# Three-stage attention and gated-MLP kernel: first query tiles issued from ScalarE, another order of the front

## The chip, the core and the metric

The kernel runs on one core of one Trainium2 chip. The metric is device time in microseconds (us) of that core. Inside the core PE (TensorE) does matmuls and transposes, DVE (VectorE), ACT (ScalarE) and POOL (GpSimd) do elementwise work, and SP (SyncE) issues DMAs. Each engine works through a queue of its own in order; a waiting instruction holds up all that stand behind it on its engine.

## What is computed

Attention with a sliding window of 16 and, beside it, one summary key and value for each block of 32; then a gated layer with a spatial matrix; then a second layer with a convolution of three taps.

```python
def _attn_ref(q, k, v):            # B=2, H=8, S=768, D=64
    k_sum = k.reshape(B, H, nb, 32, D).max(axis=3)
    v_sum = v.reshape(B, H, nb, 32, D).mean(axis=3)
    scores_l = scale * q @ k.T;  masked to abs(i - j) < 16
    scores_s = scale * q @ k_sum.T + log(32)
    a = softmax(concat(scores_l, scores_s))
    return a @ concat(v, v_sum)
def _moe_ref(x, ...):              # d_model 512, d_ff 1024
    u, v = halves of relu(x @ w_in)
    return (u * (w_spatial @ layernorm(v) + b_spatial)) @ w_out
def _moe2_ref(x, ...):
    h = relu(x @ w_in);  return (h * sigmoid(conv3(h))) @ w_out
```

## The kernel before

The attention is cut into 8 head pairs n (four for each of two batches) and each pair into two groups of six blocks of 64 queries, so there are 16 groups i. What is here called the front is the first 40 us or so: the groups of the first pairs, the loads of their keys, queries and values, and the conversion of the first weights. From then on matmuls of the gated layer ("dense" work) fill the PE between the groups.

One group (function group, L488 on) is a chain over four engines: scores on PE (L496, L503 and 24 matmuls of L509), the row maximum on DVE (L513), six exponentials with their sums on ACT (L517), the sum and its reciprocal on DVE (L520, L523), the scaling on POOL or DVE (L526), two lots of three transposes on PE (L530), each followed by a copy out of PSUM on ACT or DVE (L552), the product with the values on PE (L536), and the result split into a high part (L557, ACT or DVE) and a low part (L558, DVE). Scores of even and odd groups use two PSUM buffers in turn: scores of group i wait for the exponentials of group i - 2. All transposes share one PSUM bank, so a second lot waits for the copy of the first.

Ahead of a pair's scores stand its keys (function keys): two scaled windows of the keys, one for each group (L422 on ACT, L424 on DVE or POOL), the block maxima ("tops", L432 on DVE; two for each early pair) and their spread into place (L438). The values' block means (function means) are matmuls for pairs 0 and 2 (L452) and a DVE sum with a transpose for the others (L459, L462); ACT or DVE takes them out of PSUM (L464), and L469 (ACT) or L471 (POOL) spreads them. The first weight w_in comes in eight pieces of 64-bit words; each is converted by a scaling (L307 on ACT, L308 on POOL), three bit operations on DVE (L310, L312, L314), a cast (L298) and a subtraction (L292). The scaling takes the piece straight from its DMA.

Sizes of the loads follow from their shapes (128 partitions, 4 bytes an element): a pair's keys come as 416 and 384 columns (208 and 192 KB), its queries as two halves of 384 columns (192 KB each), its values as two pieces of 288 KB, a piece of w_in is 256 KB. All loads of before are issued by SP (L397 keys, L400 queries, L410 and L406 values, L306 weights).

The order of the work is not found by the compiler. Each job is given to a plan with add(); two tables written out in the file then decide: ORDER lists all jobs in the order in which they are emitted, two characters a job, and so sets each engine's queue; PICK says for each job that may run on several engines which one it takes. Where the plan's own estimate sees a gap of 0.5 us or more on PE it puts in filler matmuls (L1085, bf16 ones, result unused). Seven filler matmuls also stand at the very start. The estimate is used for nothing else on the chip.

Before the plan's jobs stand two DVE memsets and one exponential on ACT of a single column (L1080), which makes ACT load its table.

Of the kernel before, what the change touches and what calls it, by code (L numbers as in the profile page):

```python
# [59 lines left out]
    "EtDpEuC7C8C9C+C-BXEiDqDBCLFiEvFjE3E4EjEkDzD0EwFvCMCNDuDvCOCPD6DCDDDED7D8D9D1D+D2EEEFD3FBCQEGE5EmDFDGFkEHEIE6D4F6F7EOEPEQ"  # L60
    "ERGmD5F8F9C4FCD-EAEBECFWEXE7FFFGEYEZEaEbGnFHFIFJFKElFXEDE8GlEcEdE9FYFLGkFZFlFaGQGRGDE+ExEJEKELESHPGSGEGFEyFmE-FAFnEzFbFz"
    "F0EMFwGtG6GdEVJwFQFRFcFdF1ENHHHIGeF2F3GfGGGgF4FeHQFSFTF5FoHJFUHRGhGiGjFpFqFrGuFDG7HSHTHKHLEWFsG8GTGUGHF+GVGIFtHMHNFuFfFg"
    "HiHjFxHkHlGJFyG9G+HOHUHXHYGvGKGwHZHVFhHmHWIhGLGMF-GxGyGAHyGBHnIDHzHaGWGXImGCH0FEGoH1HbHcGYHoHqGNGZGaGbHrHsGOGcGPHdG-JtGz"
    "JuIrItIuHtIcG0H2HeGpG1HuIdIiHfIwH3GqG2IsM-INGrJxIOJzGsHvJ3HAIPHBIIHgH4HCInHDG3NBHwG4HEG5IjIvHFIXJ6IJHhJ0IEIYIKNAJ4HGNCIQ"
    "JvIeH5IZJ1IaIbIRIkIFJ5IfIxJyIyIzJBHxJCISJDHpIgILH8I0H+KbJ2H6KBJ8IlITNNKCJEH9H-IMI5H7NDKFI6IBI1I7KDIUIAIoI8JRKcJFKGI9J7NG"
    "NJJGICKHIVKXJ9JHNII2I+I3JSIWJTJUKAKYI-JJJVJIJZJaI4J-JbNEJAJcIpJKKIJWJhKEJLJdJMNFKJNHIqLDJiJeNKLHJXNUJNKQJfIGJjJ+KKJOIHKd"
    "KhJYKRJPJgLIJQKiJmKLLJJoKjNQKSJkKeNLJnLEJpJlJrLFKfKzKlKsKmKtJsKuK0KnKgKZKaLLKMLMK9KTNPLKNMK5LGKkK7LPNOLNK-K+LTNbNRKNLQNS"
    "K6NTNWLXLRLBKvLUNXLOK8LYLZLbKONVNYLVLSNiLcLdNZLALfLgLWNdLeLaKoNeLhLiNaLlLzNcKPNfLCLoL2NpLjKpNgLmNhLpNkL3NlNjLnLkL0L4MOMB"
    "NmJqKqMPMcNnKUMHL1NrNoMQNsNwKrLrNqMINtK1MEMJMRL5MCNuKVMVMdMFNzNvLqNyPXMWKWN3PLMXMDNxK3L6KwL7N0MYN1MeMmPYMnN5K4MfPMMsN2N6"
    "MGK2N4N7LvN+PZPNPaKxN8MoKyN9OAOBMKL9MzMtLsLwN-OCPbMjMuOFPOODPdOHM0PROILxPPMLMkPSOEM7OGOJMpLtPvMqPTMlMrOMPeL+OKPfPQMvOOOL"  # L70
    "OPONOTM3L-MwMxP1P2PpM4OQOUPjMMPkPUPcOaOROWMyLyOVOSMSPlOhPqM5MgM8PVPgP3PWM1MAPmMhOcM9PrOdObM6P7LuP4MZM2MiP8PnQFOXOeM+MaP5"
# [1161 lines left out]
```

## Time and profile before

| | us |
|---|---|
| median of 3 runs | 320.15 (319.69 to 320.52) |
| the profiled execution | 320.81 |
| span of its trace | 318.9 |
| PE busy in the span | 311.4 (98%) |

The span runs from the first to the last instruction of the trace; 1.9 us of the profiled execution lie around it. Busy PE time includes the filler matmuls. The views used are the busy time by engine, the busy time in stretches of the span (for all of an engine's work and for the filler alone), the instructions in order of time with what ended their waits, and the list of who waited for whom.

### The profile page before, as it was taken

How to read it: one execution, taken by the hardware profiler on the slowest of the kernel's cores; microseconds unless marked ns; L12 is line 12 of the kernel's file. 1: busy time of each engine (PE TensorE's matmuls, PEld its weight loads, DVE VectorE, ACT ScalarE, POOL GpSimd, SP SyncE). 2: the span in 40 equal slices, each digit the busy share in tenths (PEclk: the TensorE clock that was granted, in tenths of full speed). 3: DMA queues.
4: the chain of work that ended last, by engine and by line, in shares of the span. 5: the costliest groups of instructions: out<-in, count | busy, mean ns of one | idle time of the engine just before them, and what ended most of it. 6: DMA issues, size and time to landing. Idle time of an engine off the chain costs nothing.

```text
span 318.9 us, 6374 instructions
## 1 busy us (share of the span) xinstructions
PE 311.4 (98%) x2376; PEld 271.6 (85%) x2376; DVE 268.5 (84%) x493; ACT 237.3 (74%) x565; POOL 117.0 (37%) x130
## 2 busy tenths in 40 slices
PE   7899999999999999999999999999999999999994
PEld 3677889888888888999998888888888899999994
DVE  6789899886677978988987797799999999989971
ACT  3999888978385735677987687998788997684721
POOL 3597853804235337255532332210110222254010
PEclk9999999999999999999999999999999999999999
DMA  7999875935453000114434343400110412154432
GB/s 222 305 266 306 224 218 179 329 93 159 168 189 110 24 2 13 53 29 142 138 114 124 117 134 133 132 2 0 25 21 5 75 25 51 26 99 104 128 140 99
DMA packets 16061, 37.64 MB, mean 118 GB/s; under 512 B 1952, under 2 KB 8480, under 8 KB 16032
## 3 DMA queue, kind: packets, MB, share of 16 engines
q1 hardware_dynamic: 13728, 34.11, 35.0%
q0 software_dynamic: 2304, 3.15, 5.7%
q8 instruction: 18, 0.29, 0.4%
q14 instruction: 11, 0.09, 0.1%
HBM read 30.96 MB, written 3.15 MB: 107 GB/s over the span
## 4 chain that ended last, share of the span: by engine, by line
PE 88%; DVE 5%; DMA 2%; SPq 1%; ACT 1%; POOL 1%; issue 1%; DVEq 0%; POOLq 0%
PE late L345 11%; PE late L346 11%; PE late L344 11%; PE mm L344 10%; PE mm L346 9%; PE mm L345 9%; PE pt L530 3%; PE xp L344 3%; PE xp L346 3%; PE xp L345 3%; PE xp L536 3%; PE pt L344 3%; PE pt L346 3%; PE pt L345 3%; PE s L509 2%; DMA a<-q_in 2%
## 5 line engine op out<-in xcount | busy, mean ns | idle before, releaser
L517 ACT ACTIVATE a<-s,a 128x120 f32<-128x120 f32 x96 | 33.3, 379 | 1.0 <-DVE a L513 0.8
L345 PE MATMUL late<-xl,a 128*128 128x512 f32 (+1 forms) x80 | 29.5, 369 | 0.1
L344 PE MATMUL late<-xh,a 128*128 128x512 f32 (+1 forms) x80 | 29.4, 367 | 0.0
L346 PE MATMUL late<-xh,a 128*128 128x512 f32 (+1 forms) x80 | 29.4, 367 | 0.0
L914 DVE SCALAR_TENSOR_TENSOR w<-v,conv_t,w 128x1534 f32<-128x1534 f32 x12 | 21.8, 1817 | 4.4 <-POOL w L908 2.1
L876 POOL DMA_DIRECT2D tmp<-w x9 | 8.4, 931 | 42.5 <-ACT tmp L875 31.1
L526 POOL TENSOR_TENSOR a<-a,a 128x720 f32<-128x720 f32 x14 | 19.4, 1394 | 6.4 <-DVE a L523 3.5
L517 ACT ACTIVATION_READ_ACCUMULATOR a<-s,a 128x1 f32 x96 | 21.6, 225 | 0.0
L292 POOL TENSOR_TENSOR w<-a,w 128x256 fp32r<-128x256 f32 (+2 forms) x13 | 14.2, 1099 | 15.1 <-PE late L345 7.9
L530 PE MATMUL pt<-ident,a 128*120 128x128 f32 x96 | 16.5, 281 | 0.8 <-DVE a L552 0.6
L345 PEld LDWEIGHTS late<-xl,a 128*128 128x128 f32 x80 | 15.0, 188 | 2.4 <-DVE xl L292 0.4
L346 PEld LDWEIGHTS late<-xh,a 128*128 128x128 f32 x80 | 15.0, 188 | 1.9
L344 PEld LDWEIGHTS late<-xh,a 128*128 128x128 f32 x80 | 15.0, 188 | 1.8
L513 DVE TENSOR_REDUCE a<-s 128x6 f32<-128x720 f32 x16 | 14.2, 899 | 2.2 <-PE s L509 2.1
L298 ACT CAST w<-a 128x512 fp32r<-128x512 f32 (+2 forms) x17 | 10.0, 589 | 7.9 <-DVE a L337 3.4
L327 ACT ACTIVATE a<-a 128x512 uint16<-128x512 uint8 x20 | 15.8, 789 | 0.0
L330 ACT ACTIVATE a<-a 128x512 f16<-128x512 f32 x20 | 15.6, 782 | 0.0
L298 ACT CAST xh<-tmp 128x384 fp32r<-128x384 f32 x24 | 12.1, 512 | 3.9 <-DVE tmp L878 2.0
L530 PEld LDWEIGHTS pt<-ident,a 128*120 128x120 f32 x96 | 10.8, 137 | 5.0 <-DVE a L552 1.0
L344 PE MATMUL mm<-w,xh 128*128 128x512 f32 x36 | 14.9, 414 | 0.0
L344 PE MATMUL mm<-xh,a 128*128 128x512 f32 (+1 forms) x40 | 14.7, 367 | 0.0
L346 PE MATMUL mm<-xh,a 128*128 128x512 f32 (+1 forms) x40 | 14.7, 367 | 0.0
(399 smaller groups left out, 1130.8 us busy)
## 6 DMA issues: line engine op xcount, KB each, us to landing
a<-w_in SPq DMA_DIRECT2D x8, 512.0 KB, 3.5
a<-w_out SPq DMA_DIRECT2D x8, 512.0 KB, 3.5
a<-vhalf SPq DMA_DIRECT2D x8, 288.0 KB, 6.9
a<-v_in SPq DMA_DIRECT2D x6, 384.0 KB, 6.8
a<-vwin SPq DMA_DIRECT2D x4, 576.0 KB, 6.9
a<-w_in SPq DMA_DIRECT2D x8, 256.0 KB, 7.1
a<-w_inv SPq DMA_DIRECT2D x4, 512.0 KB, 4.1
a<-w_outT SPq DMA_DIRECT2D x4, 512.0 KB, 3.6
```

Source lines behind the costliest of these rows:

```text
L292: eng.tensor_tensor(out=lo.r(), in0=src.f(), in1=hi.f(), op=ALU.subtract)
L298: us = {"ACT": (0.2 + n / 1200, lambda: ACT.copy(hi.r(), src.f())), "POOL": (0.12 + n / 1050, lambda: POOL.tensor_copy(hi.r(), src.f()))}
L327: ACT.activation(out=c.ap.bitcast(U16).rearrange("p (n w) -> p n w", w=2)[:, :, 0], in_=byte, func=AF.Copy, scale=1.0 / 32.0, bias=-15.5 / ...
L330: ACT.mul(c.ap.bitcast(F16).rearrange("p (n w) -> p n w", w=2)[:, :, 1], word(), 2.0 ** -60)
L344: PE.matmul(ps, lhsT=lh, rhs=rh, start=first and i == 0, stop=False, **kinds)
L345: PE.matmul(ps, lhsT=lh, rhs=rl, start=False, stop=False, **kinds)
L346: PE.matmul(ps, lhsT=ll, rhs=rh, start=False, stop=last and i == n - 1, **kinds)
L513: DVE.tensor_reduce(out=st[:, 0], in_=sv, op=ALU.max, axis=AX.X, negate=True)
L517: ACT.activation(out=e[:, u, :NK], in_=sv[:, u // GA, u % GA], func=AF.Exp, bias=st[:, 0, u:u + 1], accum_out=sm[:, u, :1])
L526: eng.tensor_tensor(out=e, in0=e, in1=st[:, 1].unsqueeze(2).to_broadcast([128, GB, NK]), op=ALU.mult)
L530: PE.transpose(pt3[:NK, a], e[:, GA * h + a, :NK], ident)
L914: DVE.scalar_tensor_tensor(out=two(ct)[:, bs, to], in0=two(h)[:, bs, of], scalar=scale(k), in1=two(ct)[:, bs, to], op0=ALU.mult, op1=ALU.add)
```

## The change

- The two DMAs of pair 0's queries leave SP's queue and become the first two instructions of ACT's queue.
- The exponential that loads ACT's table becomes a job of the plan behind these two DMAs; the copy of the "one" tile comes after it.
- On SP's queue the second half of w_in's first chunk (issued third before) goes behind the first values; pair 1's keys move ahead of both.
- ORDER and PICK are new: 62 jobs take another engine, and the queues of PE, DVE, ACT and POOL are in another order up to the second layer's start. SP's queue is the same from the second values piece on.

```diff
             q0, q1 = S // qp * i, S // qp * (i + 1)
-            dma((q1 - q0) / 2 * 0.84 + (166 if n + i == 0 else 0), lambda ...: SP.dma_start(qts[j].ap[:, q0:q1], q_in[b, p][:, q0:q1]), r - 9 + 1.5 * i, writes=[...])
+            if n:
+                dma((q1 - q0) / 2 * 0.84, lambda ...: SP.dma_start(qts[j].ap[:, q0:q1], q_in[b, p][:, q0:q1]), r - 9 + 1.5 * i, writes=[...])
+            else:
+                add({"QA": (1.2 - 0.4 * i, lambda ...: ACT.dma_start(qts[j].ap[:, q0:q1], q_in[b, p][:, q0:q1]))}, r - 100 + i, writes=[...])
...
-    ACT.activation(out=stat[0][:, 11:12], in_=mhalf, func=AF.Exp)
...
+    def table():
+        ACT.activation(out=stat[0][:, 11:12], in_=mhalf, func=AF.Exp)
...
-    add({"ACT": (2.65, one_tile)}, -99, [tok("ident")], [mask_b.tok(sub="o")])
+    add({"ACT": (2.2, table)}, -99.5, writes=[tok("table")])
+    add({"ACT": (0.6, one_tile)}, -99, [tok("ident"), tok("table")], [mask_b.tok(sub="o")])
```

ORDER and PICK, read back into jobs, give these queues. A job is named with its pair (n) or group (i); k, q, v are loads, a and b their first and second piece; w(c, part) is a piece of w_in.

```
SP before:   k0a k0b w(0,1) q0a k1a k1b q0b v0a w(0,0) q1a v0b k2a k2b q1b ...
SP after:    k0a k0b k1a k1b v0a w(0,1) w(0,0) q1a v0b k2a k2b q1b ...      ACT: q0a q0b

ACT before:  table, one, win0/1, cast w(0,1), exp0, scale w(0,0), exp1, win2/0, exp2, mean-out0,
             copy0/1, cast w(0,0), exp3, exp4, copy2/0, hi1, copy2/1, exp5, copy3/1, scale w(2,0),
             exp6, scale w(1,0), exp7, mean-out2, spread2/0, hi3, copy4/1, win4/1, copy5/0,
             spread2/1, copy5/1, exp8, copy6/0, mean-out3, spread3/0, cast w(1,1), copy7/0,
             scale w(3,0), hi6, exp9
ACT after:   q0a, q0b, table, one, win0/0, win0/1, win1/0, exp0, scale w(0,0), exp1, cast w(0,1),
             win2/0, exp2, cast w(0,0), copy0/1, exp3, hi0, exp4, win3/0, hi1, copy2/1, exp5,
             spread1/0, copy3/1, win4/0, exp6, copy4/0, scale w(2,0), mean-out2, hi3, copy4/1,
             exp7, hi4, exp8, hi5, copy6/0, win5/0, copy6/1, spread3/0, copy7/0, spread3/1, hi6,
             copy7/1, exp9

PE before:   filler, s0, s1, mean0a, s2, mean0b, t0, s3, t0', s4, t1, pv0, t1', t2, s5, pv1, t2',
             s6, t3, mean1, t3', dense(256), s7, pv2, t4, mean2a, mean2b, t4', pv3, s8, dense(512),
             t5, pv4, t5', s9
PE after:    filler, s0, s1, mean0a, s2, mean0b, t0, s3, t0', s4, t1, pv0, t1', s5, t2, pv1, t2',
             s6, t3, mean1, mean2a, t3', s7, pv2, t4, mean2b, pv3, t4', s8, t5, pv4, t5',
             dense(512), s9

DVE before:  constants, win0/0, masks, top0a, top0b, put0, w(0,1) x3, max0, top1b, top1a, max1, ...
DVE after:   constants, masks, top0a, top0b, put0, top1a, max0, top1b, max1, w(0,1) x2, sum0, ...
```

## Rows read from the trace of the kernel before

**Rows 1.** Page, part 1: busy us, share of the span, instructions of each engine.

```profile
PE 311.4 (98%) x2376; PEld 271.6 (85%) x2376; DVE 268.5 (84%) x493; ACT 237.3 (74%) x565; POOL 117.0 (37%) x130
```

**Rows 2.** Stretches A:B: length, each engine's busy us (instructions), granted clock, DMA share, GB/s.

```profile
0.00:5.00 5.00, 3.96 (x11) 1.48 (x12) 2.70 (x23) 2.54 (x5) 1.85 (x11) 1.00 0.61 185
5.00:10.00 5.00, 4.01 (x73) 2.11 (x71) 3.31 (x8) 2.12 (x12) 2.82 (x5) 1.00 1.00 277
```

**Rows 3.** Who waited for whom on PE from 12 us on: total, times, longest.

```profile
PE pt L530 <- DVE a L552: 0.6, 1, 0.6
PE s L509 <- DMA a<-q_in: 0.3, 1, 0.3
```

**Rows 4.** In order of time, ACT's start and first issues: start, us, engine, line.

```profile
0.72 1.28 ACT L1080 ACT_TABLE_LOAD   x1 [0.72 <-PEq L1226]
0.73 0.86 SPq L397 DMA_DIRECT2D a<-k_in  x2
...
1.63 0.42 SPq L306 DMA_DIRECT2D a<-w_in  x1
...
2.10 0.43 SPq L400 DMA_DIRECT2D a<-q_in  x1
```

**Rows 5.** In order of time, the first users of loads: the bracket is the wait ended.

```profile
3.80 0.68 ACT L422 ACTIVATE a<-a 128x576 f32<-128x576 f32 x1 [1.18 <-DMA a<-k_in]
...
5.77 0.29 DVE L310 TENSOR_SCALAR a<-a 128x256 uint32<-128x256 uint32 x1 [0.40 <-DMA a<-w_in]
...
6.44 0.84 PE L509 MATMUL s<-a,a 64*64 64x120 f32 x24 [0.57 <-DMA a<-q_in]
...
10.89 0.45 ACT L307 ACTIVATE a<-a 128x256 f32<-128x256 f32 x1 [0.44 <-DMA a<-w_in]
...
12.09 0.85 PE L509 MATMUL s<-a,a 64*64 64x120 f32 x24 [0.34 <-DMA a<-q_in]
```

**Rows 6.** In order of time, from the second block maxima to the first exponentials.

```profile
4.48 0.54 DVE L432 TENSOR_REDUCE a<-a 128x12 f32<-128x384 f32 x1
...
5.06 0.31 DVE L438 TENSOR_SCALAR a<-a 128x288 f32<-128x288 f32 x1
...
8.29 0.36 ACT L517 ACTIVATE a<-s,a 128x120 f32<-128x120 f32 x1 [0.59 <-DVE a L513]
...
10.22 0.23 ACT L517 ACTIVATION_READ_ACCUMULATOR a<-s,a 128x1 f32 x1
```

**Rows 7.** Stretches between instructions of the front, columns as in rows 2.

```profile
10.89:41.94 31.05, 29.70 (x536) 23.23 (x534) 27.00 (x64) 28.86 (x123) 24.36 (x30) 1.00 0.91 259
12.09:35.52 23.43, 22.53 (x420) 17.53 (x421) 20.55 (x49) 21.83 (x97) 18.86 (x23) 1.00 1.01 296
```

**Rows 8.** The second stretch of rows 7, filler matmuls alone: PE, PEld busy.

```profile
12.09:35.52 23.43, 1.03 (x4) 0.39 (x4) 1.00 1.01 296
```

**Rows 9.** ACT's groups by shape, 10.89 to 41.94: busy us, mean ns, idle before.

```profile
L552 ACT COPY a<-pt 120x384 f32<-120x384 f32 x9 | 4.4, 485 | 0.7 <-PE pt L530 0.5
L469 ACT COPY a<-a 24x768 f32<-24x768 f32 x3 | 2.5, 829 | 0.1
L307 ACT ACTIVATE a<-a 128x256 f32<-128x256 f32 x4 | 1.9, 466 | 0.4 <-DMA a<-w_in 0.4
L557 ACT CAST xh<-xp 128x384 fp32r<-128x384 f32 x3 | 1.4, 480 | 0.8 <-PE xp L536 0.7
L422 ACT ACTIVATE a<-a 128x576 f32<-128x576 f32 x2 | 1.4, 684 | 0.0
L298 ACT CAST w<-a 128x256 fp32r<-128x256 f32 x2 | 0.8, 408 | 0.0
L464 ACT ACTIVATE a<-mm 24x128 f32<-24x128 f32 x2 | 0.5, 265 | 0.0
```

**Rows 10.** In order of time on PE, one dense step of 256 columns and what follows.

```profile
25.27 0.36 PE L344 MATMUL mm<-xh,w 128*128 128x256 f32 x1
...
25.81 0.23 PE L496 MATMUL s<-a,ones 64*64 64x72 bf16 x4
```

More of the change, by code (lines that the diff above doesn't have):

```diff
@@ L60 @@
[L60 to L71, printed above, removed]
@@ new lines @@
+    "EgBfCrBJBgBhChEiBLB3BNBKBMBiCsDTCtCXB4DfBOBtAZB5BPEfBuBvDUCiCjASCFCYC3CuDgCGB6CZBUCkCHB7DVB8DWBQClCaCICbEoCvCBCmDhCwEpCx"
+    "DsEUDiCnEqCLE1DXBRCyCoCzDYDtC0CJDjDNFPC1C4DZDaFNDbDOErDkDxCCEsDyDPDlDQDBDmC6CKDzEjFQDcEtE2AgDnFODRDuC8DdCDC7DoDeEVEuE3BV"
+    "C9DpC+BWFWDqFwBXEvE4FCDrFjEwCMC-C5EkFDE5DAD0ElD1CNE6CODvD7BYExCPFkDDDwDCF7D8D9D+DEDFCQD-E7CRF9FlE8D2EFEYDGD3D4EZD5GmD6DH"
+    "FXEGEaFGFYE9F+EbEHEcEAFmE+FHEBF8F0EIEJFIECFJFZEDGEGRFxGlFnFKEnFaE-EmFbEEEyEPGFGnEdEQFAERFBFcGSGGESEzGeEKEWEeGoF2ELFoFdET"
@@ new lines @@
+    "FRFeFLF1E0EMHQFSJxENFEGTFMFfF3FpGUHRF4GgFqGfG7GhF5GuGHEOEXGiFrHIGVFTHJF6HKFUFsGjGIFVGvHSGkG8HLHTGwFyF-GJFgHUFtFhHMFzFiG9"
+    "FuHjGAFFGxHkFvHYIdGKGBJuGLIeHlGMGyGDInGNHmIsGpGWGCGXHnIuGYIvGzHZHNHaG+G-GZIoGaHVHzGbGOHbHAGcGPGdIxG0IpHWGQG1GqH0G2HcHXIf"
+    "HOItG3H1NAGrHdHBIiIwHrHeHPGsHCHDHfJ0HEHsH2HgHoGtHFG4H3IJJ1JyIKHGHHIgITIUILJ2IMIVJ4IqHtJzJ6HhNCHuNBH4G5IWIhKCG6IjIkH5HvIl"
+    "ImHwKDKEH6NDHxKGHiKHKIIOHpNOHyIEHqIYIPIXH-INI6H9IFJ5IrNEJ3J7JKH+IZIaNHKYKcH7IQIGJ9IRJ8KZISI7KdIbJCIAIcKFJDIyNFI8I9IzICI+"
@@ new lines @@
+    "H8J+I-I0I1IDIBI2JEJFJAI3JaJGNGJSNIJTNJI4JBJUJVI5JbJLJHNKJIJWJcJdJJJiJeJXJMJNKKJjJONLKJJfJYJkKLJgKRJPKeNRJQJZJhJRJlJnKfKS"
+    "JpLIKMKgJmJoKTNQIHLEKhKaKmJqKtIINMKbLFK0JsNNJtKiKjNPKnKkNSK6KoKlKuK1NTKvK+K8LJNUK-LQLGK9LMLNLHLKLLLRK7LOLSLPLTNVLUNYNXLA"
+    "KANWNcLVLcNjLYLdKBNZLWJ-LeKNJvNaLBKULgKOLhLZLXLaKPNeLCLfLbKpNfLiLjNbLmL0KwNdKQNgLDLpL3NqLkKqNhLnNiLqNlL4NmNkLoLlL1L5MPMC"
+    "NnJrKrMQMdNoKVMIL2NsNpMRNtNxKsLsNrMJNuK2MFMKMSL6MDNvKWMWMeMGN0NwLrNzPYMXKXN4PMMYMENyK4L7KxL8N1MZN2MfMnPZMoN6K5MgPNMtN3N7"
@@ new lines @@
+    "MHK3N5N8LwN-PaPOPbKyN9MpKzN+OBOCMLL+M0MuLtLxOAODPcMkMvOGPPOEPeOIM1PSOJLyPQMMMlPTOFM8OHOKMqLuPwMrPUMmMsONPfL-OLPgPRMwOPOM"
+    "OQOOOUM4MAMxMyP2P3PqM5OROVPkMNPlPVPdObOSOXMzLzOWOTMTPmOiPrM6MhM9PWPhP4PXM2MBPnMiOdM+PsOeOcM7P8LvP5MaM3MjP9PoQGOYOfM-MbP6"
+    "PiPtOlMcQBQHQCPxMOOkL9QDOgOjPjMUMVOpQIQETYQJP+OZJwOrOsOqTZOmPuOtQKP-OhPyTeQFQAOnOwPpOuO3PzTfOvPvQYOzP7QZOyQLQdQMQeQNOxO0"
+    "QaO5QbO+O6QfO4P0QcQTQUOoQVQgO7QOQPPAOaQhQWRGO1RBPFQXQQQiPBO8PHO-QvPGP1QRQ0O9O2RLQjQkQ1Q2QqTaQwPCQrQSPIQsQtQ3PJQlQxTbQyTk"
@@ new lines @@
+    "TgRCRMQmQuRHRdQ4ThQzRDQnQ5TqTsRERNRIRYRJRORZQ6TmRaVARiRjQ7TtQoPDReTiRFR3QpTcRKRtRyTjTrRPRuRQTdUxRbTlTnT3UyRRQ8RkRzRfQ9Tu"
+    "RSRgTvR0RlR4T4UsPKRUQ+RvPLR5RTR1ToRcQ-RhRmRwR6U2RnSHSMSNT7TpRASCRVSgSDR2RxR7PETwTxR8SEU3SFRoSIRWRpRrRqSGU7R9SJR+R-SAUzSO"
+    "SKSbSLScShRXSPRsU8SdVBSBTDSiSRTQTSSeSQTRU9SSSUSlSTTIU0SVSjSWUtS0SmS+SXVCU4U1SnSfS5TTUuSoTKSYVLSZSkSqVMTLSaTyS6TJVESrSpSs"
+    "VDTES1UvStS-U+VFS2S3TMVNSuSvSwVWSyS7S8TUUYVPVHTNTVSxU5USUMUeTOS4UmUNVQSzVIU6UZTFUfUTVOUgTAUwT5S9TPUOVXUaVGVhVSUUVYWBVZVs"
@@ new lines @@
+    "UkU-TWVdTGViUVVTV8UWUPVeTBWCT8VJUQV9V4V0V5VRUqVKTHVuVjVaVUTXVkVoV1VcWxV2UoWyV6VVTzT0VfVwV7VpV3VnV+VgWDVlT+WEWzXAWFXBV-UA"
+    "UbT6WAUFW2VbWsWNWOW3WGXCUHVmUBWHUnWIUIW0W1WPUlWQWtT1WJVqUhXLVrVtUrWRUiXMWaUpWKT2XETCWbW7W4WLWUWuXNUcW5XDWvWcXFW8WwXHXIXW"
+    "XPWVWdW9W6WWXOXQXhWXXwXXXYX0XSX4YBWSX5WgT-XGVvX8XTX1T9X6WmUCXZW+YCXiWTXdUdXaUDW-VyXRXjXsWnXeXkX2VxX9WhXoUEX3XJYDX7XpVzUG"
+    "X+WiYEXlYFXuXKX-WoYAXmYNXbYOWYYGUJWMYHURWeUKXcULYPXvYIXyXtYJXUWpYQYKXfYUYLXVYRXxYSWjXzWqXnXqWkYaYgYmXgYnUjYhUXWZYMYoYTYp"
@@ L399, in load_kq @@
             q0, q1 = S // qp * i, S // qp * (i + 1)
-            dma((q1 - q0) / 2 * 0.84 + (166 if n + i == 0 else 0), lambda q0=q0, q1=q1: SP.dma_start(qts[j].ap[:, q0:q1], q_in[b, p][:, q0:q1]), r - 9 + 1.5 * i, writes=[qts[j].tok(q0, q1)])
+            if n:
+                dma((q1 - q0) / 2 * 0.84, lambda q0=q0, q1=q1: SP.dma_start(qts[j].ap[:, q0:q1], q_in[b, p][:, q0:q1]), r - 9 + 1.5 * i, writes=[qts[j].tok(q0, q1)])
+            else:
+                add({"QA": (1.2 - 0.4 * i, lambda q0=q0, q1=q1: ACT.dma_start(qts[j].ap[:, q0:q1], q_in[b, p][:, q0:q1]))}, r - 100 + i, writes=[qts[j].tok(q0, q1)])
     def load_values(n):
```

22 lines of the change are left out of this document (5 added, 17 removed).

## The prediction

> **What bounds the kernel now.** I read the busy time by engine first: PE is busy for 98% of the span [rows 1], so what a change of the front can win is time in which PE does nothing useful. Next I read the list of PE's waits after 12 us: apart from 0.3 us for queries and 0.6 us for a copy on DVE it holds nothing worth a tenth per cent [rows 3]. The matmuls after the front are dense, so each microsecond by which the front's useful PE work is done sooner should reach the end of the run, and each new hole in it too. The loss is thus in the front, and in two parts. Up to 12.09 us PE does scores of two groups and half a block mean; the second pair's queries end that part [rows 5]. From 12.09 us to the tenth group's scores (s9) at 35.52 us, PE is busy for 22.53 of 23.43 us, of which 1.03 us is filler [rows 7, 8]: 21.50 us of work, 1.93 us lost.
>
> Then I asked what else is full there. The DMA engines are: their share is 1.00 from 5 to 10 us, at 277 GB/s, after a first stretch of 0.61 that includes the time before the first issue at 0.73 us [rows 2, 4]. ACT is nearly full: from 10.89 us, when a piece of w_in lets its scaling start [rows 5], to the start of exp9 at 41.94 us it works for 28.86 of 31.05 us and is idle for 2.19 us [rows 7]. So two limits stand beside PE: the bytes that must land, and ACT's one queue.
>
> **The change, part by part: the queries on ACT's queue.** Before, the first query piece was issued at 2.10 us behind keys and a weight piece, and s0's big matmuls started with it at 6.44 us after a wait of 0.57 us [rows 4, 5]. Now it is issued at about 0.7 us beside the first keys. No trace shows a DMA issued from ACT; the nearest rows are SP's 0.43 us each [rows 4]. Twice that is 0.86 us ahead of the table load, which moves from 0.72 to about 1.6 us. ACT's first need of data came at 3.80 us after a wait of 1.18 us [rows 5], so this is hidden; with that cover gone it would cost 0.86 us.
>
> What the queries gain, the keys lose. Both key pieces, 400 KB, had landed by 3.80 us, three pieces (656 KB) by 5.77 us, four (848 KB) by 6.44 us [rows 5]. Now 784 KB compete (two of keys, two of queries). Let L be the landing of the second key piece. Read off between 656 KB and 848 KB, L is 6.27 us; counted from 400 KB at 3.80 us with 277 GB/s [rows 2, 5], 0.393 MB take 1.42 us and L is 5.2 us. I take the middle, 5.75 us. From it the chain is: block maxima and spread, 4.48 to 5.37 us before [rows 6], 0.89 us; s0 and the row maximum, from 6.44 to 8.29 us [rows 5, 6], 1.85 us; exp0, 8.29 to 10.45 us [rows 6], 2.16 us; together 4.90 us. So s0's matmuls start at 6.1 to 7.2 us (before 6.44), and exp0 ends at L + 4.9, that is 10.1 to 11.2 us. s1 no longer waits, and follows.
>
> **What does not move.** Behind exp0 on ACT stands, before and after, the scaling of w(0,0), and behind that exp1. The scaling started at 10.89 us, when its piece landed [rows 5]. In the old order the pieces up to and with it are k0a, k0b, w(0,1), q0a, k1a, k1b, q0b, v0a, w(0,0), 1984 KB. In the new order they are the same nine pieces, on two queues. With the same DMA engines full, the piece lands at the same time and exp1 starts at about 11.24 us again, provided that exp0 is done, which holds for L below 5.99 us; at L = 6.27 us it is 0.28 us late. The second pair's queries, 192 KB behind, also have the same bytes ahead of them, so s2 stays at about 12.09 us. What is won ahead of 12 us by earlier s0 and s1 is then lost again in these two waits: I count it at nothing, with 0.28 us of loss as the other bound, and a gain as in the first rival.
>
> **The new order after that.** The most it can win by s9 is the 1.93 us lost there now. ACT's queue decides how much comes, since s9 needs the buffer that exp7 reads. In the new order there stand from exp1 to exp7 seven groups of exponentials at 2.16 us (15.1), two casts at 0.41 (0.8), three key windows at 0.68 (2.1), five copies at 0.485 (2.4), three high parts at 0.48 (1.4), one spread at 0.83, one scaling at 0.47 and one mean at 0.27 [rows 6, 9]: 23.4 us. Without any hole exp7 ends at 11.24 + 23.4 = 34.7 us, and s9 starts then. Before, s9 started at 35.52 us, but PE had done one dense step of 256 columns more, 0.54 us from 25.27 to 25.81 us [rows 10]. So the gain is 35.52 - 34.7 - 0.54 = 0.3 us. If ACT's neighbours overlap by about 0.1 us each it is more; a hole on ACT makes it less. It lies between 0.9 and -0.5 us, which I take from half a microsecond of such overlap or of holes on either side.
>
> The other moved jobs are costed at nothing: the three bit operations of w(0,1) on DVE wait for a piece that lands four us later, but only the cast on ACT behind exp1 and dense steps after 30 us need them. POOL has ten jobs fewer; DVE gets them, with 268.5 us busy of 318.9 us [rows 1]. If DVE lost that cover, each moved job would cost some 0.4 us (its bit operation takes 0.29 us [rows 5]).
>
> **Sum.** The profiled execution took 320.81 us, 318.9 us of it span; the 1.9 us around it stay. 318.9 - 0.3 = 318.6 us of span, 320.5 us in all. That execution is 0.66 us above the median of the runs, 320.15 us, so the forecast median is 320.15 - 0.3 = 319.85, say 319.9 us.
>
> **Rivals.** First, the queries on a queue of their own cost the others nothing, and all that SP issues lands sooner. The nine pieces then count 1600 KB; 384 KB at 277 GB/s [rows 2] are 1.4 us, ACT's chain starts at about 9.8 us, and the gain is 1.7 us: 318.4 us. For it speaks the share of 0.61 in the first five us, part of which may be room that a second queue fills; against it the full 1.00 right behind [rows 2]. The Trainium skill ("DMA: Bandwidth & Descriptors", section "Issuing engines are not separate DMA queues") says that DMAs of ACT and SP run on the same 16 engines and interleave, and that a second issuer saves issue time only. It speaks against this rival, as the full share does; by it the sum stays at the forecast.
>
> Second, the slower side: ACT becomes the bound. Between exp1 and exp9 the new queue holds, against the old, three high parts (1.44), three windows (2.05), two spreads (1.66), three copies (1.46) and a cast (0.41) more, 7.0 us, and two means (0.53), three copies (1.46), two scalings (0.93), two spreads (1.66), a window (0.68) and a cast (0.41) less, 5.7 us, by the same durations [rows 9]. That is 1.35 us more. ACT was idle for 2.19 us there [rows 7]; if the new order leaves it idle for more than 0.84 us, exp9 comes later than at 41.94 us, and if it is idle for as long as before, by 1.35 us, with PE's transposes behind it: 320.15 + 1.35 = 321.5 us. For it speaks that most of ACT's idle time was waiting for PE's transposes and products [rows 9], which a new order need not remove; against it that PE has dense steps between its groups from 33 us on.
>
> Third, the change does not do what it says: the table load goes first and the queries are issued at about 2 us, as before [rows 4]. The keys then land as before, and the bound by w(0,0) is the same: 320.1 us, with the order's part alone.
>
> **Chances.** Forecast 0.45, first rival 0.25, second 0.22, third 0.08. About 0.3%, 0.96 us, can be told from no change, so the borders are 319.2 and 321.1 us. Faster: 0.05 of the forecast and 0.22 of the first rival, 0.27. Slower: 0.04 of the forecast and 0.16 of the second, 0.20. Within: 0.53. The range from 318.4 to 321.5 us takes in the sum's ends (319.2 to 320.7) and reaches to the centres of both rivals.
>
> **What would show it.** Right, if the scaling of w(0,0) starts within 0.4 us of 10.89 us and s2 within 0.4 us of 12.09 us, with the keys' second piece at 5.2 to 6.3 us and s9 at 34 to 35.5 us. The first rival shows in a scaling at about 9.5 us; the second in ACT idle for over 0.84 us between them and exp9 past 42 us; the third in a table load ahead of the DMAs. I am wrong if PE's waits or filler after 36 us exceed half a microsecond, or if s0's 24 matmuls take much over 0.84 us at a granted clock of 1.00 [rows 2, 5], since less filler stands before them.

## The result: slower

| | before | after |
|---|---|---|
| median of 6 runs, us | 320.53 (319.69 to 322.13) | 323.98 (322.49 to 327.81) |
| the profiled execution | 320.81 | 324.33 |
| span of its trace | 318.9 | 322.4 |

The ratio after to before is 1.0102 [1.0056, 1.0148]; it leaves out the run of 327.81 us, which fell in a slower state. The brackets are intervals of 95%. A second measurement of the unaltered changed kernel, in the last experiment, gave 322.38 us and 1.0054 [1.0029, 1.0079]. The two overlap between 1.0056 and 1.0079; I take it that the change costs somewhat over half a per cent. The forecast was 319.9 us with a range up to 321.5 us, and it put the likeliest outcome at no change that can be told.

First the page of the changed kernel, part 1 (busy us, share, instructions), which answers [rows 1]:

```profile
PE 313.8 (97%) x2382; PEld 271.9 (84%) x2382; DVE 279.5 (87%) x503; ACT 236.8 (73%) x565; POOL 110.2 (34%) x120
```

PE is busy 2.4 us longer with 6 instructions more: fillers, 28 instead of 22. DVE has ten instructions more and is busy 11.0 us longer; POOL has ten less and is busy 6.8 us less. These are net numbers. The two PICK tables differ for 66 jobs (not 62, as the section on the change has it): 17 go from POOL to DVE and 9 back, 14 from ACT to DVE and 12 back, 8 from POOL to ACT and 6 back. So 11.0 against 6.8 us is not the price of ten jobs.

Then the loads, in order of time, against [rows 4, 5]; the bracket is the wait that the instruction ended with:

```profile
0.72 0.89 ACTq L403 DMA_DIRECT2D a<-q_in  x2
0.72 1.80 SPq L397 DMA_DIRECT2D a<-k_in  x4
1.64 1.28 ACT L1116 ACT_TABLE_LOAD   x1 [1.64 <-PEq L1232]
...
4.81 0.56 DVE L435 TENSOR_REDUCE a<-a 128x12 f32<-128x384 f32 x1 [0.70 <-DMA a<-k_in]
...
5.40 0.31 DVE L441 TENSOR_SCALAR a<-a 128x288 f32<-128x288 f32 x1
...
11.64 0.46 ACT L307 ACTIVATE a<-a 128x256 f32<-128x256 f32 x1
```

The second key piece had landed at 4.81 us, and the keys' maxima were in place at 5.71 us. The scaling of w(0,0) at 11.64 us no longer waits for its DMA: it follows the six exponentials of exp0 without a break. The stretches of [rows 2], for the changed kernel (length, busy us by engine, granted clock, DMA share, GB/s):

```profile
0.00:5.00 5.00, 3.96 (x10) 1.48 (x11) 2.19 (x22) 2.74 (x6) 1.85 (x11) 1.00 0.64 212
5.00:10.00 5.00, 5.00 (x80) 2.98 (x79) 2.49 (x6) 1.56 (x5) 0.67 (x1) 1.00 1.04 321
```

In ten microseconds 2.67 MB are moved (5 x 212 and 5 x 321), against 2.31 MB before. The front is better fed; how much of this is the change and how much the execution, the queries alone show below. What PE does with it stands in its own timeline:

```profile
1.04 6.66 PE L1087 MATMUL mm<-ones 128*128 128x512 bf16 x17 [1.04 <-DVE mhalf L1082]
...
7.81 0.79 PE L512 MATMUL s<-a,a 64*64 64x120 f32 x24
...
11.83 0.23 PE L499 MATMUL s<-a,ones 64*64 64x72 bf16 x4 [0.29 <-ACT a L520]
...
11.99 0.81 PE L512 MATMUL s<-a,a 64*64 64x120 f32 x24
```

Seventeen fillers stand ahead of s0, where before had thirteen, and they last until 7.70 us. The keys had been ready for two microseconds by then. So s0 starts at 7.81 us (6.44 before [rows 5]), exp0 at 9.62 us (8.29 [rows 6]), and s2 waits for exp0's buffer. Who waited for whom on PE from 12 us on (total, times, longest), against [rows 3]:

```profile
PE mm L455 <- DMA a<-vhalf: 1.0, 1, 1.0
PE xp L465 <- DVE xl L561: 0.9, 1, 0.9
PE xp L539 <- issue: 0.4, 1, 0.4
PE xp L539 <- DVE a L526: 0.4, 1, 0.4
PE late L344 <- DVE a L751: 0.3, 1, 0.3
PE s L499 <- ACT a L520: 0.3, 1, 0.3
PE pt L533 <- ACT a L555: 0.2, 1, 0.2
```

That is 3.5 us. [rows 3] hold 0.9 us, and the same list of before has a third row, 0.2 us for values, so 1.1 us in all. The two largest are a block mean that waits for its values at 25.68 us and a transpose of pair 5's value sums at 67.22 us that waits for DVE. The stretches that answer [rows 7], for ACT from the scaling to exp9 (11.64 to 44.08 us) and for PE from s2 to s9 (11.99 to 37.10 us):

```profile
11.64:44.08 32.44, 30.30 (x536) 23.33 (x535) 29.77 (x68) 29.96 (x126) 23.82 (x28) 1.00 0.77 228
11.99:37.10 25.11, 23.26 (x436) 17.69 (x432) 23.32 (x54) 22.99 (x105) 19.22 (x23) 1.00 0.93 269
```

And the filler alone in the second, as in [rows 8]:

```profile
11.99:37.10 25.11, 2.24 (x8) 0.62 (x8) 1.00 0.93 269
```

From s2 to s9 filler fills 2.24 us instead of 1.03 us. Last, what goes on around the wait at 67.22 us, DVE and POOL in order of time:

```profile
63.49 1.58 POOL L292 TENSOR_TENSOR w<-a,w 128x512 fp32r<-128x512 f32 x1
...
63.83 2.00 DVE L529 TENSOR_TENSOR a<-a,a 128x720 f32<-128x720 f32 x1
65.76 0.94 DVE L462 TENSOR_REDUCE a<-a 128x24 f32<-128x768 f32 x1
66.62 0.54 DVE L561 TENSOR_TENSOR xl<-xp,xh 128x384 fp32r<-128x384 f32 x1
...
67.22 0.28 PE L465 MATMUL xp<-ident,a 128*24 128x128 f32 x1 [0.90 <-DVE xl L561]
```

The scaling of group 11 (L529) was POOL's before; the new PICK gives it to DVE. There it takes 2.00 us beside a subtraction on POOL. Behind it on DVE's queue stand the value sum (L462) and a low part (L561), and PE's transpose waits for these.

### The profile page after: what moved, and what is told of

It reads as the page before. It is cut to its first block, busy times and chain, and to the rows that moved or that the text cites. A ratio compares the mean times of both kernels' runs of the same rounds, so it can differ in the third digit from the quotient of the medians.

```text
span 322.4 us, 6405 instructions
## 1 busy us (share of the span) xinstructions
PE 313.8 (97%) x2382; PEld 271.9 (84%) x2382; DVE 279.5 (87%) x503; ACT 236.8 (73%) x565; POOL 110.2 (34%) x120
## 4 chain that ended last, share of the span: by engine, by line
PE 76%; DVE 12%; ACT 4%; POOL 3%; issue 2%; DMA 2%; DVEq 0%; POOLq 0%; ACTq 0%
PE late L345 9%; PE late L344 9%; PE late L346 9%; PE mm L344 8%; PE mm L346 7%; PE mm L345 7%; PE pt L533 3%; PE mm L1087 2%; PE xp L539 2%; PE xp L345 2%; PE xp L346 2%; PE xp L344 2%; PE pt L346 2%; PE pt L344 2%; PE pt L345 2%
## 5 line engine op out<-in xcount | busy, mean ns | idle before, releaser
L345 PE MATMUL late<-xl,a 128*128 128x512 f32 (+1 forms) x80 | 29.5, 369 | 0.1
L346 PE MATMUL late<-xh,a 128*128 128x512 f32 (+1 forms) x80 | 29.4, 367 | 0.0
L520 ACT ACTIVATION_READ_ACCUMULATOR a<-s,a 128x1 f32 x96 | 22.5, 234 | 0.0
L529 POOL TENSOR_TENSOR a<-a,a 128x720 f32<-128x720 f32 x12 | 16.8, 1400 | 15.1 <-DVE a L526 11.2
L345 PEld LDWEIGHTS late<-xl,a 128*128 128x128 f32 x80 | 15.0, 188 | 2.3 <-DVE xl L292 0.4
L346 PEld LDWEIGHTS late<-xh,a 128*128 128x128 f32 x80 | 15.0, 188 | 1.9
L555 ACT COPY a<-pt 120x384 f32<-120x384 f32 x20 | 9.8, 491 | 8.5 <-PE pt L533 8.2
L346 PE MATMUL mm<-xh,a 128*128 128x512 f32 (+1 forms) x40 | 14.7, 367 | 0.0
L345 PE MATMUL mm<-xl,a 128*128 128x512 f32 (+1 forms) x40 | 14.7, 367 | 0.0
```

The costliest lines, as they stand in the source:

```text
L345: PE.matmul(ps, lhsT=lh, rhs=rl, start=False, stop=False, **kinds)
L346: PE.matmul(ps, lhsT=ll, rhs=rh, start=False, stop=last and i == n - 1, **kinds)
L520: ACT.activation(out=e[:, u, :NK], in_=sv[:, u // GA, u % GA], func=AF.Exp, bias=st[:, 0, u:u + 1], accum_out=sm[:, u, :1])
L529: eng.tensor_tensor(out=e, in0=e, in1=st[:, 1].unsqueeze(2).to_broadcast([128, GB, NK]), op=ALU.mult)
L555: (ACT.copy if eng is ACT else DVE.tensor_copy)(part.ap[:NK], pt[:NK, :128 * GA])
```

## The experiments

The theories were these. **Filler:** the plan's own estimate puts seventeen fillers ahead of s0, four more than before, and the front's gain is spent on them. **Order:** the new ORDER and PICK make holes later, whatever the front does; within it, the wait at 67 us and the values at 25 us were suspects. **Loads:** the queries on ACT's queue delay or speed the other loads, and with them the scaling of w(0,0). **Clock:** with less filler PE's slow start costs as much as the filler did. In the expectations quoted below, Theory A is Filler, B and F are Order, C is Loads, D is filler and order together, and G is Clock. Each ratio below is to the kernel before on the same chip. In the diffs, FILLS replaces the estimate by fixed numbers of fillers, by job; job 43 is s0, and seven more fillers stand at the very start in all kernels.

### Less filler ahead of s0 (e1_filler), and the changed kernel without the new queue (e2_order_alone)

```diff
# e1: the changed kernel
+FILLS = {43: 3, 99: 3, 49: 3, 156: 2, 107: 3}
-                if self.fill and gap >= 0.5:
-                    n = int((gap - 0.1) / 0.22)
+                if self.fill and FILLS.get(k, 0):
+                    n = FILLS.get(k, 0)
# e2: the changed kernel, 17 fillers (43: 10), and
-            if n:
+            if True:   # pair 0's queries by SP too; loads and table load in before's order
```

> The changed kernel with 3 instead of 10 filler matmuls added behind the seven of the start, so 10 instead of 17 stand before the first scores; all else, the later filler too, is as in the changed kernel. Theory A (the filler holds the front): in the changed kernel the keys were spread at 5.71 us, but the first big score matmuls started at 7.81 us behind 17 fillers; here they start at 5.9 to 6.1 us, exp0 at about 7.8 us instead of 9.62 us, exp1 at 11.0 to 11.4 us instead of 11.97 us, and the time falls by 0.6 to 1.5 us, to 322.5 to 323.4 us. Theory B (the new order behind 12 us loses the time): s0 starts sooner, but the time stays within 0.5 us of 323.98 us.

> The changed kernel's order and engine choices with the loads as before: the first queries on SP's queue again, the piece of w_in third; the numbers of filler matmuls are those of the changed kernel (17 before s0). Theory B (the new order loses the time): 323 to 325 us, with the hole on PE ahead of the third pair's block means (0.96 us) and that at 66 us (0.9 us) still there. Rival C (the loads lose it, because keys, values or weights land later): back to 320.0 to 321.0 us.

e1 took 321.49 us, 1.0031 [1.0015, 1.0047], a larger gain than Theory A expected; e2 took 323.24 us, 1.0075 [1.0048, 1.0101], as Theory B expected. In e1 everything in front comes sooner (PE and ACT in order of time):

```profile
1.04 3.68 PE L1088 MATMUL mm<-ones 128*128 128x512 bf16 x10 [1.04 <-DVE mhalf L1083]
...
5.85 0.85 PE L513 MATMUL s<-a,a 64*64 64x120 f32 x24 [0.84 <-ACT a L426]
...
9.73 0.45 ACT L308 ACTIVATE a<-a 128x256 f32<-128x256 f32 x1
...
10.07 0.81 PE L513 MATMUL s<-a,a 64*64 64x120 f32 x24
```

s0 is two microseconds sooner than in the changed kernel, s2 too, and s9 starts at 33.76 us against 35.70 us before. Yet the kernel is slower than before. So filler is a part of the loss and not all of it, and what else costs lies behind s9. e2 says that it does not hang on the queue: with the old loads the new order is slower all the same.

### The queries alone (e3_queries_alone, e7_queries_filler)

```diff
# e3: the kernel before with the change's q0a, q0b and table jobs; old order of all else, 13 fillers
-SP: k0a k0b w(0,1) q0a k1a k1b q0b v0a ...   ACT: table, one, ...
+SP: k0a k0b w(0,1) k1a k1b v0a ...           ACT: q0a, q0b, table, one, ...
# e7: e3 with 10 fillers ahead of s0
```

> The order and engine choices of before with nothing but the first queries moved to ACT's queue ahead of the table load; the piece of w_in stays third on SP's queue, the filler numbers stay those of before (13 in front of s0). Theory B: 319.8 to 320.8 us, no change; s0 starts at 5.6 to 6.4 us instead of 6.44, s2 at 12.1 us as before. Rival C (the queries' loads cost the rest): 321.5 us or more, with s2 later than 12.6 us. A third view (they help by themselves): below 319.6 us.

> e3_queries_alone (the order of before, the first queries on ACT's queue) with 10 instead of 13 filler matmuls in front of s0. Theory A in its general form (filler in front of s0 costs as soon as the scores could start before it ends, and how long it takes depends on when PE's clock rises in that execution): 319.7 to 320.4 us, and the times spread less than the 319.97 to 322.20 us of e3_queries_alone. Rival: the filler is hidden there, 320.5 to 321 us with the same spread.

e3 took 320.70 us, 1.0001 [0.9976, 1.0026], as Theory B expected; e7 took 320.31 us, 1.0007 [0.9978, 1.0037], and its times spread over 319.71 to 323.05 us, where a smaller spread than e3's was expected. These are e3's stretches up to 10 us:

```profile
0.00:5.00 5.00, 3.96 (x12) 1.52 (x13) 2.26 (x23) 1.94 (x5) 1.85 (x11) 1.00 0.64 210
5.00:10.00 5.00, 4.87 (x84) 3.06 (x81) 4.59 (x10) 2.48 (x11) 3.01 (x5) 1.00 1.05 319
```

The trace of before alone is not enough to compare with. In e8, below, all loads are issued by SP in the order of before and only the filler differs; its stretches are:

```profile
0.00:5.00 5.00, 3.96 (x11) 1.49 (x12) 2.72 (x23) 2.54 (x5) 1.85 (x11) 1.00 0.60 164
5.00:10.00 5.00, 5.00 (x81) 2.94 (x80) 3.64 (x9) 1.97 (x10) 3.10 (x5) 1.00 1.02 319
```

All traces together, one for each kernel:

| first queries issued by | traces | 0 to 5 us, GB/s | 5 to 10 us, GB/s | MB in 10 us |
|---|---|---|---|---|
| SP | before, e2, e6, e8 | 141 to 185 | 277 to 331 | 2.31 to 2.42 |
| ACT | the 13 others | 210 to 218 | 295 to 361 | 2.52 to 2.89 |

So the issue from ACT feeds the first five microseconds better in every trace, by 0.26 MB in the mean (5 us at 213 instead of 161 GB/s). The higher rate behind 5 us does not come from it: e8 has it without.

When the scaling of w(0,0) can start is less clear. It ran without a wait at 10.56 us in e3 and 10.23 us in e7, but at 10.47 us in e8 too. The three lines are of e6 (loads by SP) and e12 (queries by ACT, below), where it waited for its piece, and of e8, where it did not:

```profile
10.70 0.44 ACT L308 ACTIVATE a<-a 128x256 f32<-128x256 f32 x1 [0.38 <-DMA a<-w_in]
11.39 0.44 ACT L308 ACTIVATE a<-a 128x256 f32<-128x256 f32 x1 [0.41 <-DMA a<-w_in]
10.47 0.45 ACT L308 ACTIVATE a<-a 128x256 f32<-128x256 f32 x1
```

The same holds behind it: s2 comes at 10.90 us in e3 (12.09 before [rows 5], 11.16 in e8) and s9 at 35.01 us (35.70 before, 34.94 in e8). At s9 e3's trace is no further ahead of before's than e8's is, and the times show no difference: a gain of the queue alone is neither shown nor excluded.

### The wait for the values (e4_means_late)

```diff
# the changed kernel, 17 fillers, on PE:
-... mean1, mean2a, t3', s7, pv2, t4, mean2b, pv3, ...
+... mean1, t3', s7, pv2, t4, pv3, mean2a, mean2b, ...
```

> The changed kernel with the two lots of block-mean matmuls of the third pair moved on PE's queue behind the product of group 3; filler and all else as in the changed kernel. Theory B, part one (PE stands 0.96 us for the third pair's values, which land later than the order supposes): the hole ahead of those matmuls goes, s7 starts about 1 us sooner (26.7 instead of 27.75 us), and the time falls by 0.5 to 1.0 us, to 323.0 to 323.5 us. Rival: other holes (ACT's copies, DVE) take its place and the time stays within 0.4 us of 323.98 us.

It took 325.29 us, 1.0132 [1.0101, 1.0163]: worse, and outside both expected ranges. The wait for the values is gone, and PE's list holds two others, of 1.8 and 1.4 us; what lies behind them was not followed up:

```profile
PE xp L540 <- POOL w L299: 1.8, 1, 1.8
PE pt L534 <- DVE a L556: 1.4, 1, 1.4
```

The wait itself is not steady: 1.0 us in the changed kernel's trace, not in the list of its second one (e15), and 1.5 us in e14's. I leave it as a part of the spread between executions.

### The front alone and the rest alone (e5_front_alone, e6_rest_alone)

```diff
# e5: 10 fillers
-ORDER, PICK: the changed kernel's
+ORDER, PICK: the changed kernel's up to exp9 (loads and ACT's queue with them), before's behind it
# e6: the other way round
+ORDER, PICK: before's up to exp9, the changed kernel's behind it
```

> The changed kernel's loads, order and engine choices up to the exponentials of group 9 and, for all jobs behind, the order and engine choices of before; 10 filler matmuls stand before s0 as in e1_filler. Theory D (two causes: the filler ahead of s0, and the order behind the front; the changed front itself gains): the gain that e1_filler showed at s9 (33.76 against 35.70 us, less one dense step of 0.54 us: 1.4 us) is kept to the end: 318.8 to 319.8 us, ratio 0.994 to 0.998. Rival E (the later order loses nothing; the front's lead is only work put off): 321 to 322 us as in e1_filler.

> Loads, order, engine choices and filler of before up to the exponentials of group 9; for all jobs behind, the changed order and engine choices. Theory D: the later order loses 1.3 to 2.3 us by itself: 321.8 to 323 us, with PE holes of 0.5 us or more at 55 to 70 us that before has not. Rival E: 320.0 to 321.0 us, no change.

e5 took 319.88 us, 0.9969 [0.9950, 0.9988]: faster than both kernels, and within the ratio that Theory D expected. Its s0 starts at 5.84 us and its s9 at 34.48 us. From 12 us on PE's waits are two (ahead of that it also waits 1.0 us for the first values):

```profile
PE xp L540 <- issue: 0.4, 1, 0.4
PE pt L534 <- ACT a L556: 0.2, 1, 0.2
```

e6 took 324.51 us, 1.0119 [1.0079, 1.0158], slower than expected, but it does not price the rest of the order: where the two orders meet, PE waits 2.2 us for a copy on ACT (`PE pt L534 <- ACT a L556: 2.2, 1, 2.2`), which neither kernel has.

### Filler in the other kernels (e8_filler_before, e9_front_filler17, e12_front_filler7)

```diff
# e8: the kernel before, 17 fillers ahead of s0 instead of 13
+FILLS = {42: 10, 55: 5, 104: 4}
# e9: e5 with 17;  e12: e5 with the 7 at the start alone
-FILLS = {43: 3, 99: 3, 49: 3, 156: 2, 107: 3}
+FILLS = {43: 10, 99: 3, 49: 3, 156: 2, 107: 3}
+FILLS = {99: 3, 49: 3, 156: 2, 107: 3}
```

> The kernel before with 17 instead of 13 filler matmuls in front of s0, nothing else changed. Its first queries land at 6.4 us; 17 fillers ended at 6.6 to 7.6 us in the changed kernel and its relatives. Theory A: s0 starts 0.3 to 1.3 us later than 6.44 us, by when the clock rises, and the time is 0.2 to 0.9 us longer, 320.7 to 321.5 us, with a wider spread. Rival (filler is hidden because ACT's chain waits at 10.9 us for a piece of w_in in any case): no change, 320.2 to 320.8 us.

> e5_front_alone with the changed kernel's 17 instead of 10 filler matmuls in front of s0, nothing else. Theory A: the filler's price is the same in this kernel as in the changed one (323.98 against 321.49 us, 2.5 us): 321.7 to 322.7 us against 319.88 us, s0 at 6.6 to 7.9 us by when PE's clock rises. Rival: with the later order of before, which had no hole behind 45 us, dense work takes up the delay and less than 1 us is lost: 320.0 to 320.9 us.

> e5_front_alone with no filler ahead of s0 but the seven of the start, which end at 4.1 us at the latest; s0 starts at 5.84 us in any case, since its keys are spread then. Theory A: filler below ten is not in the way and changes nothing as long as PE's clock rises in time: 319.4 to 320.2 us. Rival G (an idle PE from 4.1 to 5.8 us delays the rise of its clock, so that s0, s1 and the block means run at the lower level): s0's matmuls take more than 1.2 us instead of 0.85, and the time is 0.5 to 1.5 us longer, 320.4 to 321.4 us.

e8: 321.20 us, by the ratio 1.0004 [0.9985, 1.0023] no change, as its rival said. The old front's s0 waits for its loads until 6.44 us anyway [rows 5], and with four fillers more it starts at 6.60 us. e9: 320.72 us, 1.0001 [0.9976, 1.0026]: seven fillers more take away what e5 had won, which is near the rival's price and not Theory A's 2.5 us. e12: 320.77 us, 1.0011 [0.9999, 1.0024]: three less take it away too. Its PE timeline shows a reason:

```profile
1.04 3.17 PE L1088 MATMUL mm<-ones 128*128 128x512 bf16 x7 [1.04 <-DVE mhalf L1083]
...
6.19 1.48 PE L513 MATMUL s<-a,a 64*64 64x120 f32 x24 [1.53 <-ACT a L426]
...
7.71 1.46 PE L513 MATMUL s<-a,a 64*64 64x120 f32 x24
```

After seven fillers and 1.53 us of idling, s0 and s1 take 1.48 and 1.46 us, where e5's take 0.85 and 0.82 us. The granted clock reads 1.00 in this stretch, so only the pace tells the level: s0 takes 1.7 times as long as in e5, which fits the lower of PE's two levels, 1.2 GHz, at which the seven fillers ran (512 columns in 0.43 us). The 1.3 us lost on s0 and s1 are about as much as the 0.42% between e12 and e5; this trace also has a late piece of w_in (11.39 us, above), the cause of which is open. So the filler is not waste: enough of it is needed ahead of s0, and what exceeds that delays s0. Ten are near the edge: in e11 and e13, below, with ten, s0 still took 1.28 and 1.12 us.

### The wait at 67 us (e10_hole, e11_norm_pool)

```diff
# e10: e1, on PE
-..., mean5 transpose, t11, dense, dense, ...
+..., dense, dense, mean5 transpose, t11, ...
# e11: e1, PICK of one job (scaling of group 11)
-DVE
+POOL
```

> e1_filler (the changed kernel with 10 filler matmuls) with the transpose of pair 5's block means and the first transposes of group 11 moved on PE's queue behind two dense steps of 512 columns. Theory F (the later order's loss is the holes on PE that its trace shows: 0.9 us at 63 us, 0.4, 0.4 and 0.2 us elsewhere): the hole at 63 us goes and the time falls by 0.6 to 0.9 us, to 320.6 to 320.9 us. Rival (the loss lies in how full DVE is, so the hole comes back one step later): 321.2 to 321.7 us.

> e1_filler with one engine choice undone: the scaling of group 11 on POOL again instead of DVE. On DVE it took 2.00 us beside a subtraction on POOL of 1.57 us, where other such scalings took 0.90 us, and the low part for which PE stood 0.9 us at 63 us was queued behind it. Theory F with this cause: the hole shrinks to 0.3 us or less, 320.6 to 321.0 us. Rival: the scaling ends later on POOL (1.4 us, behind two subtractions) and the transposes of group 11 wait instead: 321.3 to 322 us.

e10 took 321.42 us, 1.0035 [1.0012, 1.0057], no gain to be seen over e1's 1.0031, and in the rival's range: the 0.9 us wait is gone and s15 starts 1.0 us sooner than in e1, but another wait of 0.4 us stands later (`PE mm L346 <- DVE w L293: 0.4, 1, 0.4`), and from s15 to the end it takes 253.0 us where e1 takes 252.3 us. Moving the wait away on PE alone did not help; DVE's queue is as full as in e1. e11 took 320.58 us, 1.0002 [0.9981, 1.0023], at the lower edge of Theory F's range. With the scaling back on POOL the value sum and the low part come sooner on DVE, and PE's transpose does not wait:

```profile
59.38 1.39 POOL L530 TENSOR_TENSOR a<-a,a 128x720 f32<-128x720 f32 x1
...
61.61 0.94 DVE L463 TENSOR_REDUCE a<-a 128x24 f32<-128x768 f32 x1
62.48 0.54 DVE L562 TENSOR_TENSOR xl<-xp,xh 128x384 fp32r<-128x384 f32 x1
...
63.07 0.28 PE L466 MATMUL xp<-ident,a 128*24 128x128 f32 x1
```

One job's engine is worth 0.29% by this pair.

### The new order up to 67 us, and the sum (e13_cut_late, e14_norm_pool17, e15_changed_again)

```diff
# e13: e11 with before's ORDER and PICK for the jobs behind exp15 (about 67 us)
# e14: the changed kernel, 17 fillers, with group 11's scaling on POOL
# e15: the changed kernel as it is
```

> e11_norm_pool (the changed kernel with 10 filler matmuls and group 11's scaling on POOL) with the order and engine choices of before for all jobs behind the exponentials of group 15, about 67 us on. e11_norm_pool stood at 1.0002 and e5_front_alone, with the old order from 42 us on, at 0.9969. If the rest of the loss lies behind 67 us (0.4 us at a low part's sum on DVE behind 100 us is the only hole on PE left there): 0.996 to 0.999, 319.4 to 320.2 us. If it lies between 42 and 67 us: 1.000 to 1.002, 320.5 to 321.2 us.

> The changed kernel with its 17 filler matmuls and only group 11's scaling put back on POOL. If the prices add (filler 2.3 us as between the changed kernel and e1_filler, scaling 0.9 us): 322.6 to 323.5 us, ratio 1.006 to 1.009. If the filler costs 1.0 us, as between e5_front_alone and e9_front_filler17, and more only by shifting the later order into the scaling's collision: 321.3 to 322.0 us, ratio 1.002 to 1.005.

> The changed kernel unaltered (its filler numbers written out as constants), beside the two others on one chip, since the interval of its first measurement is wide (1.0056 to 1.0148). Expected 1.007 to 1.011, 322.8 to 324.2 us. Below 1.006 the price of the filler, taken from it and e1_filler, would have been overstated and be nearer to the 1.0 us seen without the new later order.

e13 took 319.82 us, 0.9967 [0.9950, 0.9985], as fast as e5. e14 took 321.74 us, 1.0022 [0.9997, 1.0047], in the lower of its two ranges, and e15 322.38 us, 1.0054 [1.0029, 1.0079], below what was expected; both put the seven fillers nearer to 1 us than to 2.3 us. In per cent of 320.6 us the parts are:

| part | from | difference | us |
|---|---|---|---|
| the new front, 10 fillers, group 11's scaling on POOL | e13 (e5: -0.31) | -0.33 [-0.50, -0.15] | -1.1 |
| the new order behind 67 us | e11 - e13 | +0.35, uncertain by 0.27 | +1.1 |
| group 11's scaling on DVE | e1 - e11, e15 - e14 | +0.29, +0.32 | +1.0 |
| seven more fillers ahead of s0 | e15 - e1, e14 - e11, e9 - e5 | +0.23, +0.20, +0.32 | +0.8 |

A single difference of two ratios is uncertain by about 0.3 (root of the sum of the squares of two half intervals of 0.16 to 0.25). The three of the filler together give 0.25 with 0.18, the two of the scaling 0.30 with 0.22, so both are clear of zero. From e13 over e11 and e1 the parts lead to e15 by construction; that e5, e9 and e14 agree with them was not built in.

The 1.1 us behind 67 us is not located. From s15 to the end of the span e11 takes 252.0 us and e13 251.5 us, 0.6 us less; 0.4 us of this is a wait that e11 has and e13 has not (`PE late L345 <- DVE a L752: 0.4, 1, 0.4`). The rest stays open; it may be no more than the uncertainty of the difference.

One experiment is missing: the new front with ten fillers and all loads issued by SP as before. So the 1.1 us that the front wins are not divided between the queries' queue and the new order. With the order of before the queue shows no gain (e3, e7), and with the new order and seventeen fillers none that can be told (e2 at 1.0075, e15 at 1.0054).

## Why the prediction was wrong

Two losses that the sum put at nothing made the kernel slower: the filler ahead of s0 (0.8 us), and the jobs moved behind the front (1.0 us for one of them, and about 1.1 us, uncertain, for the order behind 67 us). A gain that it put at nothing, the time that SP's issues take one behind the other, was real but smaller. Part by part:

**What bounds the kernel: right.** PE bounds it, and time won in the front does reach the end: e5 is 1.0 us faster, and its trace, 0.7 us ahead at s9 (34.48 against 35.70 us, less one dense step of 0.54 us), is 0.8 us shorter. That each new hole reaches the end was said too, and the holes came.

**The issue of the queries: right.** Two issues took 0.89 us (forecast 0.86), the table load followed at 1.64 us (1.6), and ACT still waited 0.56 us for its keys, so the cover held. The third rival, a table load first, is out.

**The landing of the keys, and s0: failed, twice.** L was 4.81 us, ahead of the 5.2 to 6.3 us forecast, so s0 could have started at 5.85 us, as e1 shows, ahead of the 6.1 to 7.2 us forecast. It started at 7.81 us because of the filler. The text named the filler only as a sign, with the wrong sign: "less filler stands before them". The front's description says that the number follows the plan's own estimate; what that estimate makes of the new order had to be worked out before anything else in the front. I costed the code that the diff shows and not the code that its tables make the plan emit.

**The scaling of w(0,0) "fixed" at 10.89 us: failed.** It rested on the same nine pieces landing at the same time whichever queue issues them. With the queries on ACT's queue the piece had landed by 9.73 us in e1 and by 9.41 us in e10, where the loads of before had it wait until 10.89 and 10.70 us (before, e6). The mechanism of the first rival is there, and in e1 in about the size that it gave (1.16 us sooner, 1.4 us forecast), but it is not steady: e8 had the piece by 10.47 us with the loads of before, and e12 only at 11.39 us with the new ones. The row on which I dismissed the rival, a DMA share of 1.00 from 5 to 10 us, was beside the point: what the queue fills is the first stretch, with its share of 0.61. The Trainium skill ("DMA: Bandwidth & Descriptors", section "Issuing engines are not separate DMA queues") says that a second issuer saves issue time only, and I read it as no gain. The saving that it grants, two issues of 0.43 us [rows 4], would be an estimated 0.24 MB at 277 GB/s [rows 2]; the traces show 0.26 MB more in the first five microseconds, so they agree with the page. The step that failed was to set issue time at nothing while the DMA engines had room before 5 us. s2 at 11.99 us was within the forecast's 0.4 us of 12.09 us for the wrong reason: it waited for exp0's buffer, and comes at 10.07 us where s0 is sooner.

**The order up to s9: the size was luck.** Forecast was a gain of 0.3 us between the scaling and s9, with 0.54 us of dense work put behind. In e15 that stretch is 35.44 - 11.42 = 24.02 us, in e1 33.76 - 9.73 = 24.03 us; before, the 24 matmuls of s9 started at 35.70 us, so it was 35.70 - 10.89 = 24.81 us, less the dense step 24.27 us: a gain of 0.25 us. But in the other traces with the old order up to s9 (e3, e6, e7, e8) the stretch is 24.40 to 24.47 us, less the dense step 23.9 us, and no gain is left. Nor did ACT's queue decide when s9 starts: in e1 exp7 ended at 32.82 us, and PE was then at work on a transpose and a dense step until s9's first matmuls at 33.58 us. What e1 is ahead at s9 it has won ahead of the scaling. The profiled execution of the changed kernel lost 1.0 us to the values in the same stretch.

**The second rival, ACT as the bound: the sign came, the mechanism did not.** exp9 came after 42 us in the changed kernel (44.08) with ACT idle for 2.48 us of 32.44. But in e1, with the same order on ACT, the stretch from the scaling to exp9 takes 31.00 us, and in e15 30.99 us, against 31.05 us before [rows 7]. ACT works for 29.87 us of it in e1, 1.01 us more than before, and is idle for 1.13 us instead of 2.19 us. The later exp9 is the later start, by the filler, and the wait for the values. That rival's place and price were not what made the kernel slower.

**The other moved jobs "costed at nothing": failed, and the largest miss.** The text bounded each by 0.4 us if DVE's cover went, from the shortest bit operation. One of them, group 11's scaling, cost 1.0 us, and the rest of the order behind 67 us perhaps as much. The scaling of 720 columns took 0.9 us on DVE before when it ran there:

```profile
L526 DVE TENSOR_TENSOR a<-a,a 128x720 f32<-128x720 f32 x2 | 1.8, 905 | 0.0
```

That row of before (DVE by shape up to 130 us: busy us, mean ns), beside the 1.39 us that POOL takes for the same shape, was the bound to take, not a bit operation's 0.29 us. And behind it the order of DVE's queue had to be read up to the next PE instruction that waits for it. I did that for the front alone and stopped at s9, with 66 jobs on other engines, 40 of them behind exp9.

**The sum.** A gain of 0.3 us was forecast; the front with ten fillers gave about 1.0 us. What turned it round is 0.8 us of filler, 1.0 us of one job on another engine, and about 1.1 us of the rest (uncertain by 0.9 us and not located), of which I had counted none.

## What to carry to other kernels

Where a table or an estimate decides what is emitted, work out what it emits before pricing the edit: here the estimate put seven fillers more than the ten that served best (of seven, ten and seventeen) into a front that the edit had made ready sooner. When jobs change engine, price each on its new engine by the row of the same shape, and follow that engine's queue to the next instruction of the bounding engine, over the whole kernel and not the part that the change is about. A searched order can be good in one part and bad in another: cut it, keep the part that pays (here up to exp9 or up to 67 us, 0.9969 and 0.9967), and leave the rest as it was.
